# Placing a group's output stage inside the second batch's attention, and transposing the late batches' rows on TensorE

## The chip, the cores and the metric

The kernel runs on one core of one Trainium2 chip. The metric is device microseconds of that core; three runs of the kernel before gave 349.78, 351.61 and 352.11 us, with the median at 351.61.

## The reference

For each of 8 batches and 8 heads (576 tokens, head dimension 64) the reference computes causal attention with a window of 128 tokens and a linear position bias, then feeds the rows to a two-layer block with a gated activation:

```python
scores = scale * (q @ k.T) + slope[h] * -(i - j)      # only 0 <= i - j < 128
attn   = softmax(scores);  x = attn @ v               # heads side by side: 4608 x 512
h      = x @ w_in                                     # 512 x 2048
out    = (h / (1 + exp(-beta * h))) @ w_out           # 2048 x 512
```

## The kernel before, in words

**Tiling.** The 4608 token rows form 9 groups of 512 (`TOKG`). A group needs 16 H items (`HS(g, j)`: four matmuls of 128x512 through `W1`, L507, then a tanh on ScalarE, L514, and a gate on VectorE, L515, into `gts[g]`) and 16 O items (`OS(g, i, n)`: four matmuls through `W2`, L530, for row block i; the fourth item of a block also scales it into `osb` on ScalarE, L536). A finished block is stored by `store()`, L543, nearly always from GpSimd's queue. The H items read the transposed attention output `XT`, a ring of three groups.

**Attention.** Batches 0 and 1 work on head pairs: `TP` transposes q and k on TensorE (L288), `SP_` forms scores in the PSUM tile `SS` and takes the exponential (L341), `PVP` multiplies with v (L364) and normalizes, `XP` puts the pair into `XT` (L375). The visit "A" of a pair covers the first two query blocks, and "B" query blocks 2 and 3, which read key and v blocks 1, 2 and 3. The last 64 rows of a batch have steps of their own, `tail(b)`: `TT`, `SCT`, two `PV` and `X`. Batches 2 to 7 have q and k transposed by DMA (`DT`, L403), scores by `SC` (L424, exponentials L434, mask L438), `PV` (L459, L463, L348, L349), and `X`, which carries a block of rows into `XT`. For batches below `XDMA` = 4, X is four TensorE transposes into PSUM (L482) and a copy on VectorE (L488); from batch 4 on it is one DMA transpose, issued by SyncE (L477).

**Loads.** `get` and `get_pair` issue q, k and v from SyncE's queue into the `fst` buffers (13 of them). GpSimd casts them to bf16: `cast_pair`, `cast_qk` (L252, L253) and `cast_v` (L265). GpSimd's queue also loads the weights with a cast on the way (`load_w1`, L272; `load_w2`, L276: four pieces of four O steps each), makes the masks (`constants_masks`, L195) and issues the stores.

**What sets the order.** TensorE, SyncE and GpSimd execute in exactly the order in which the program emits their instructions; ScalarE's and VectorE's order is written out only for the opening, and is planned by the framework after that. After the opening, batch 1's attention and batch 0's last rows (the list `second`, 23 steps) are spread over the H items 3 to 15 of group 0. Then comes group 1: its H items with all O items of group 0 and the first half of its own, `tail(1)` and batch 2's loads (`jobs(2)`) in between. From there on each group g has its 16 H items, half of the O items of group g-1 and half of its own; `spread` sets the steps of the batches 2 to 7 (`att`) between them by weight, from item `first` to item `last`, so that the rows of the next group are complete in time (`need`).

Of the kernel before, what the change touches and what calls it, by code (L numbers as in the profile page):

```python
# [15 lines left out]
P = 128  # L16
# [3 lines left out]
def kernel(  # L20
# [10 lines left out]
    nc = tc.nc  # L31
# [7 lines left out]
    NQB = 5  # L39
# [8 lines left out]
    qscale = 1.0 / sqrt(D)  # L48
    REF = 63.5
    FAR = 1.0e5  # L50
    XDMA = 4

    const = ctx.enter_context(tc.tile_pool(name="const", bufs=1))
    ident = const.tile([P, P], BF16, name="ident")
# [26 lines left out]
    fst_pool = ctx.enter_context(tc.tile_pool(name="fst", bufs=13))  # L81
    bst_pool = ctx.enter_context(tc.tile_pool(name="bst", bufs=4))
    pt_pool = ctx.enter_context(tc.tile_pool(name="ptp", bufs=10))
    xn_pool = ctx.enter_context(tc.tile_pool(name="xn", bufs=4))
    gt_pool = ctx.enter_context(tc.tile_pool(name="gt", bufs=2))
    sig_pool = ctx.enter_context(tc.tile_pool(name="sig", bufs=3))
    osb_pool = ctx.enter_context(tc.tile_pool(name="osb", bufs=4))
# [187 lines left out]
    def load_w2(n):  # L275
        return nc.gpsimd.dma_start(  # L276
            out=W2[:, bass.ts(n, 4), :], in_=W2v[:, bass.ts(n, 4), :])
# [191 lines left out]
    def X(b, qb):  # L469
        nq = ROWS[qb]  # L470
        xnv = xns.pop((b, qb))[:].rearrange("p h d -> p (h d)")
        if b >= XDMA:
            tok0 = (b * S + P * qb) % XTR
            n1 = min(nq, XTR - tok0)
            for r0, r1, at in ((0, n1, tok0), (n1, nq, 0)):
                if r0 < r1:
                    nc.sync.dma_start(  # L477
                        out=XT[:, :, at : at + r1 - r0], in_=xnv[r0:r1], transpose=True)
            return
        xt = psum_t.tile([P, NDM, P], BF16, name="xt", tag="t")  # L480
        for c in range(NDM):
            nc.tensor.transpose(  # L482
                out=xt[:, c, 0:nq], in_=xnv[0:nq, c * P : (c + 1) * P],
                identity=ident[0:nq, 0:nq]
            )
# [33 lines left out]
    def HS(g, j):  # L519
        Hm(g, j, range(NDM))  # L520
# [37 lines left out]
    def pvx(b, qbs):  # L558
        r = []
        for qb in qbs:  # L560
            r += [(None, lambda g=g, qb=qb: PV(b, qb, g), 2) for g in range(2)]
            if b >= XDMA:
                r.append(((b, qb), lambda qb=qb: X(b, qb), 0))
            elif qb != qbs[0]:
                r.append(((b, qb - 1), lambda qb=qb: X(b, qb - 1), 2))
        if b < XDMA:
            r.append(((b, qbs[-1]), lambda: X(b, qbs[-1]), 2))
        return r

    def merged(a, c):  # L570
# [35 lines left out]
    with tc.manual_schedule(engines={ENG.PE, ENG.SP, ENG.Pool}):  # L606
# [66 lines left out]
        for n in range(1, NP):  # L673
            get_pair(1, n)
            if n == 1:
                get("v", 1, 0)
                get("v", 1, 1)
        get("v", 1, 2)
        get("v", 1, 3)
        for b in range(2):  # L680
            for w in "qkv":
                get(w, b, 4)
        cast_pair(1, 0)
        cast_pair(1, 1)
        cast_v(1, 0)
# [2 lines left out]
        w2 = [load_w2(0), load_w2(1)]  # L688
        cast_pair(1, 3)
        w2 += [load_w2(2), load_w2(3)]  # L690
        cast_v(1, 2)
        cast_v(1, 3)
        for b in range(2):
            cast_qk(b, 4)
            cast_v(b, 4)
        constants_masks()
        second = [
            lambda: TP(1, 0), lambda: SP_(1, "A", 0), lambda: (TP(1, 1), SP_(1, "B", 0)),
            lambda: SP_(1, "A", 1), lambda: PVP(1, "A", 0), lambda: (TP(1, 2), SP_(1, "B", 1)),
# [3 lines left out]
            lambda: (XP(1, 1), PVP(1, "B", 2)), lambda: PVP(1, "A", 3), lambda: XP(1, 2),  # L703
            lambda: PVP(1, "B", 3), lambda: XP(1, 3),
        ] + tail(0)
        done = 0
        for j in range(3, NFF):
            HS(0, j)
            to = len(second) * max(0, j + 1 - 5) // (NFF - 5)
            while done < to:  # L710
                second[done]()
                done += 1


        work = tail(1)
        b2 = jobs(2)
        after_w2 = [True]
        for n in range(5):
            s, j = b2.pop(0)
            r = j()  # L720
            if after_w2[0]:
                after_w2[0] = False
                after(r[0], w2[1])
        OG = lambda g, i: [lambda n=n: OS(g, i, n) for n in range(4)]
        HG = lambda g: [lambda j=j: HS(g, j) for j in range(NFF)]
        h = HG(1)
        items = h[:4]
        o = OG(0, 0) + OG(0, 1) + OG(0, 2) + OG(0, 3) + OG(1, 0) + OG(1, 1)
        for n in range(12):
            items += [h[4 + n]] + o[n : n + 1]  # L730
        items += o[12:]
        done, dw, dj = 0, 0, 0

        def spread(items, first, last, target):
# [13 lines left out]
        def wrap(it, n):  # L748
            def f():
                nonlocal dw, dj  # L750
                it()
                while dw < min(len(work), len(work) * (n + 1) // 10):
                    work[dw]()
                    dw += 1
                while dj < min(len(b2), len(b2) * (n + 1) // 24):
                    b2[dj][1]()
                    dj += 1
            return f

        spread([wrap(it, n) for n, it in enumerate(items)], 17, len(items) - 2, need[2])  # L760
        for g in range(2, NTG):
            h = HG(g)
            o = OG(g - 1, 2) + OG(g - 1, 3)
# [41 lines left out]
```

The softmax here doesn't subtract the row's maximum and nothing guards it: scores larger than these inputs give would overflow.

## Time and profile before

| | |
|---|---|
| median of three runs | 351.61 us (349.78 to 352.11) |
| profiled execution | 352.11 us, span of the instructions 350.1 us |
| PE busy | 324.5 us, 93% of the span |
| DVE / ACT / POOL busy | 192.3 / 206.9 / 111.5 us |
| H matmuls, L507, on `hps` | 560 recorded, 382 ns each |
| O matmuls, L530 | 576, 379 ns each |
| X on TensorE, L482 | 48 matmuls, from 60.5 to 154.8 us |
| X by DMA, L477 | 21 DMA transposes, from 163.4 to 305.7 us |
| stores from GpSimd's queue | 34 of 256 KB |

In the profile PE is TensorE's matmuls, PEld its weight loads, DVE VectorE, ACT ScalarE, POOL GpSimd, SP SyncE; a name such as L507 is a line of the kernel. A busy time counts the modelled lengths of matmuls, which overlap in a stream: in the chain of waits, four matmuls of 512 columns in a row follow each other within 0.86 us. A row of a timeline gives the start and the length in us, engine, line, operation, output and inputs with their shapes, and in brackets the idle time ahead of it with what ended it. The slices of the page divide the span into 40 equal parts, one digit (tenths) each.

### The profile page before, as it was taken

The numbers are of one execution on the slowest core, as the hardware profiler recorded it, in microseconds if no ns is written. First come the engines' busy times: TensorE is split into PE (matmuls) and PEld (weight loads), VectorE is DVE, ScalarE is ACT, GpSimd is POOL, SyncE is SP. The second block draws the span as 40 slices with busy tenths as digits, with TensorE's granted clock in tenths as the row PEclk, the third lists the DMA queues.
The fourth block names the chain that finished last, engine by engine and source line by source line (L and its number), as shares of the span: only waits on it lengthen the run. The fifth ranks groups of instructions, "written<-read, shape, count | busy, mean of one in ns | idle before, by whom it ended". The sixth has DMA issues, their size and how long they took to land.

```text
span 350.1 us, 6218 instructions
## 1 busy us (share of the span) xinstructions
PE 324.5 (93%) x2289; PEld 151.4 (43%) x2289; DVE 192.3 (55%) x422; ACT 206.9 (59%) x396; POOL 111.5 (32%) x208
## 2 busy tenths in 40 slices
PE   6886886998999999998999999999999999999995
PEld 2442443443444444443444444444444444544442
DVE  7445576454754776476627763674477455614500
ACT  2545663548856776566657775675687566426511
POOL 4793624633735333503131324242200100010010
PEclk9899999899999999999999999999999999999999
DMA  7998999999999999991286989799311201120012
GB/s 176 228 195 204 194 186 202 177 201 220 217 230 237 239 211 226 212 198 48 57 182 133 182 175 227 129 222 166 93 32 53 77 30 47 30 99 0 30 62 90
DMA packets 152285, 51.79 MB, mean 148 GB/s; under 512 B 143664, under 2 KB 149824, under 8 KB 152256
## 3 DMA queue, kind: packets, MB, share of 16 engines
q1 hardware_dynamic: 145312, 38.30, 57.5%
q0 software_dynamic: 6944, 13.11, 14.9%
q8 instruction: 18, 0.29, 0.4%
q14 instruction: 11, 0.09, 0.1%
HBM read 36.71 MB, written 9.44 MB: 132 GB/s over the span
## 4 chain that ended last, share of the span: by engine, by line
PE 67%; ACT 11%; DVE 10%; DMA 6%; issue 3%; SPq 3%; POOL 0%; POOLq 0%; ACTq 0%
PE ops L530 31%; PE hps L507 26%; ACT pt L434 8%; DVE gT L515 4%; DVE pt L438 4%; PE SS L424 3%; DMA W<-in_moe_w_in_dram 3%; ACT sig L514 2%; SPq L234 2%; DMA fst<-in_k_dram 2%; PE pv L463 2%; PE pv L459 1%; DMA fst<-in_q_dram 1%; DVE xn L349 1%; PE SS L324 1%
## 5 line engine op out<-in xcount | busy, mean ns | idle before, releaser
L507 PE MATMUL hps<-XT,W 128*128 128x512 bf16 x560 | 141.5, 382 | 5.6 <-DVE gT L515 4.0
L530 PE MATMUL ops<-W,gT 128*128 128x512 bf16 x576 | 139.0, 379 | 0.0
L515 DVE SCALAR_TENSOR_TENSOR gT<-sig,hps 128x512 bf16<-128x512 bf16 x140 | 94.7, 683 | 76.4 <-ACT sig L514 75.7
L514 ACT ACTIVATE sig<-hps,beta_h 128x512 bf16<-128x512 f32 x140 | 95.8, 694 | 61.4 <-PE hps L507 56.1
L434 ACT ACTIVATE pt<-SS,bias 128x256 bf16<-128x256 f32 (+1 forms) x192 | 75.0, 478 | 11.4 <-PE SS L424 11.3
L507 PEld LDWEIGHTS <-W 128*128 128x128 bf16 x576 | 51.5, 98 | 62.6 <-issue 11.8
L530 PEld LDWEIGHTS <-gT 128*128 128x128 bf16 x576 | 52.4, 98 | 58.1 <-issue 2.1
L543 POOL DMA_DIRECT2D out_dram<-osb x34 | 18.4, 542 | 136.2 <-ACT osb L536 134.4
L438 DVE TENSOR_TENSOR pt<-pt,mask 128x1024 bf16<-128x1024 bf16 x48 | 38.0, 792 | 26.7 <-ACT pt L434 26.7
L536 ACT ACTIVATE osb<-ops 128x512 f32<-128x512 f32 x36 | 21.6, 600 | 44.6 <-PE ops L530 44.6
L265 POOL CAST vs<-fst 128x512 bf16<-128x512 f32 (+1 forms) x40 | 25.0, 636 | 37.4 <-DMA fst<-in_v_dram 32.5
L252 POOL CAST bst<-fst 128x512 bf16<-128x512 f32 (+1 forms) x32 | 20.7, 647 | 32.5 <-DMA fst<-in_q_dram 22.9
L349 DVE TENSOR_TENSOR xn<-pv,zs 128x256 bf16<-128x256 f32 (+1 forms) x64 | 26.9, 421 | 1.7
L348 DVE RECIPROCAL zs<-pv 128x4 f32<-128x4 f32 (+1 forms) x80 | 14.0, 176 | 22.3 <-PE pv L463 13.3
L253 POOL CAST bst<-fst 128x512 bf16<-128x512 f32 (+1 forms) x32 | 21.0, 656 | 10.2 <-DMA fst<-in_k_dram 10.0
L463 PE MATMUL pv<-vs,pt 128*128 128x65 bf16 x240 | 21.4, 193 | 0.0
L424 PE MATMUL SS<-qkT 64*128 64x256 bf16 (+2 forms) x240 | 18.9, 252 | 2.6 <-ACT pt L434 2.4
L463 PEld LDWEIGHTS <-pt 128*128 128x128 bf16 x240 | 16.5, 97 | 8.4
L341 ACT ACTIVATE pt<-SS 128x768 bf16<-128x768 f32 (+1 forms) x12 | 10.6, 881 | 15.5 <-PE SS L335 15.4
L424 PEld LDWEIGHTS <-qkT 64*128 64x128 bf16 x240 | 8.4, 94 | 23.1 <-issue 22.7
L459 PE MATMUL pv<-vs,pt 128*128 128x65 bf16 x192 | 17.9, 193 | 0.0
L459 PEld LDWEIGHTS <-pt 128*128 128x128 bf16 x192 | 15.2, 98 | 5.6
(78 smaller groups left out, 148.5 us busy)
## 6 DMA issues: line engine op xcount, KB each, us to landing
out_dram<-osb POOLq DMA_DIRECT2D x34, 256.0 KB, 3.3
fst<-in_q_dram SPq DMA_DIRECT2D x32, 256.0 KB, 4.8
fst<-in_v_dram SPq DMA_DIRECT2D x32, 256.0 KB, 4.0
fst<-in_k_dram SPq DMA_DIRECT2D x24, 256.0 KB, 5.2
fst<-in_k_dram SPq DMA_DIRECT2D x24, 128.0 KB, 4.0
W<-in_moe_w_in_dram POOLq DMA_DIRECT2D x4, 512.0 KB, 9.5
W<-in_moe_w_out_dram POOLq DMA_DIRECT2D x4, 512.0 KB, 11.1
fst<-in_q_dram SPq DMA_DIRECT2D x8, 128.0 KB, 3.3
```

What stands on the lines that cost most here:

```text
L265: return nc.gpsimd.tensor_copy(out=VS[b % 2][0:rows, sb, :, 0:D], in_=fs.pop(("v", b, sb))[0:rows])
L349: nc.vector.tensor_tensor(out=xn, in0=pv[0:nq, :, 0:D], in1=zs[0:nq].broadcast_to([nq, 4, D]), op=ALU.mult)
L424: nc.tensor.matmul(o, lhsT=qk[64 * e : 64 * e + 64, 1, p, P * kb : P * kb + P], rhs=qk[64 * e : 64 * e + 64, 0, p, P * kb : P * kb + nq], ...
L434: nc.scalar.activation(out=pt[:, e, cols], in_=sps[:, e, cols], func=ACTF.Exp, scale=qscale, bias=bias[:, half, h : h + 1],)
L438: nc.vector.tensor_tensor(out=pt[:], in0=pt[:], in1=masks[m][:], op=ALU.mult)
L459: nc.tensor.matmul(pv[:, hl, 0 : D + 1], lhsT=weights(b, qb - 1, h, 1), rhs=vs[:, qb - 1, h, 0 : D + 1], start=True, stop=False,)
L463: nc.tensor.matmul(pv[:, hl, 0 : D + 1], lhsT=weights(b, qb, h, 0), rhs=vs[:, qb, h, 0 : D + 1], start=qb == 0, stop=True,)
L507: nc.tensor.matmul(hps[:], lhsT=W1[:, c, bass.ts(j, P)], rhs=XT[:, c, c0 : c0 + TOKG], start=(c == 0), stop=(c == NDM - 1),)
L514: nc.scalar.activation(out=sig[:], in_=hps[:], func=ACTF.Tanh, scale=beta_h[:, j : j + 1])
L515: nc.vector.scalar_tensor_tensor(out=gts[g][:, j, :], in0=sig[:], scalar=1.0, in1=hps[:], op0=ALU.add, op1=ALU.mult)
L530: nc.tensor.matmul(ops_, lhsT=gT[:, j, i * P : i * P + P], rhs=W2[:, j, :], start=(j == 0), stop=(j == NFF - 1),)
L536: nc.scalar.mul(osb[:], ops_, 0.5)
```

## The change

- `second` is spread over 21 items in place of 13: H items 3 to 15 of group 0, and then the eight O items of its row blocks 0 and 1, alternating. Finished blocks are stored there.
- Group 1 has its 16 H items with the eight O items of group 0's row blocks 2 and 3 between them, and then the first half of its own O items. `att` starts after item 10 in place of 17.
- SyncE issues q, k, v of batch 0's last rows ahead of the last two v blocks of batch 1, and GpSimd casts in the same order; the masks are made ahead of batch 1's first cast.
- Batch 2's ten q and k loads are issued in one go; its casts, DMA transposes and v loads follow in a list of their own, spread over group 1.
- X is done on TensorE and VectorE for all batches; `XDMA` and the DMA transposes of `X` are gone. `att` now ends three items before a group's end in every group, where it was seven in the groups with X by DMA.
- `xn` has 3 buffers in place of 4.

```diff
-    XDMA = 4
...
-    xn_pool = ctx.enter_context(tc.tile_pool(name="xn", bufs=4))
+    xn_pool = ctx.enter_context(tc.tile_pool(name="xn", bufs=3))
...
     def X(b, qb):
         nq = ROWS[qb]
         xnv = xns.pop((b, qb))[:].rearrange("p h d -> p (h d)")
-        if b >= XDMA:
-            tok0 = (b * S + P * qb) % XTR
-            n1 = min(nq, XTR - tok0)
-            for r0, r1, at in ((0, n1, tok0), (n1, nq, 0)):
-                if r0 < r1:
-                    nc.sync.dma_start(
-                        out=XT[:, :, at : at + r1 - r0], in_=xnv[r0:r1], transpose=True)
-            return
...
             r += [(None, lambda g=g, qb=qb: PV(b, qb, g), 2) for g in range(2)]
-            if b >= XDMA:
-                r.append(((b, qb), lambda qb=qb: X(b, qb), 0))
-            elif qb != qbs[0]:
+            if qb != qbs[0]:
                 r.append(((b, qb - 1), lambda qb=qb: X(b, qb - 1), 2))
-        if b < XDMA:
-            r.append(((b, qbs[-1]), lambda: X(b, qbs[-1]), 2))
+        r.append(((b, qbs[-1]), lambda: X(b, qbs[-1]), 2))
...
+        for w in "qkv":
+            get(w, 0, 4)
         get("v", 1, 2)
         get("v", 1, 3)
-        for b in range(2):
-            for w in "qkv":
-                get(w, b, 4)
+        for w in "qkv":
+            get(w, 1, 4)
+        constants_masks()
         cast_pair(1, 0)
...
         w2 += [load_w2(2), load_w2(3)]
+        cast_qk(0, 4)
+        cast_v(0, 4)
         cast_v(1, 2)
         cast_v(1, 3)
-        for b in range(2):
-            cast_qk(b, 4)
-            cast_v(b, 4)
-        constants_masks()
+        cast_qk(1, 4)
+        cast_v(1, 4)
+        for sb in range(NQB):
+            r = get("q", 2, sb)
+            if sb == 0:
+                after(r, w2[1])
+            get("k", 2, sb)
...
+        fills = HG(0)[3:]
+        for n in range(4):
+            fills += [OG(0, 0)[n], OG(0, 1)[n]]
         done = 0
-        for j in range(3, NFF):
-            HS(0, j)
-            to = len(second) * max(0, j + 1 - 5) // (NFF - 5)
+        for n, f in enumerate(fills):
+            f()
+            to = len(second) * max(0, n - 2) // (len(fills) - 3)
             while done < to:
                 second[done]()
                 done += 1
+            if waiting:
+                store()
...
-        items = h[:4]
-        o = OG(0, 0) + OG(0, 1) + OG(0, 2) + OG(0, 3) + OG(1, 0) + OG(1, 1)
-        for n in range(12):
-            items += [h[4 + n]] + o[n : n + 1]
-        items += o[12:]
+        o = OG(0, 2) + OG(0, 3)
+        items = []
+        for n in range(8):
+            items += h[2 * n : 2 * n + 2] + o[n : n + 1]
+        items += OG(1, 0) + OG(1, 1)
...
-                while dj < min(len(b2), len(b2) * (n + 1) // 24):
-                    b2[dj][1]()
+                while dj < min(len(b2), len(b2) * (n + 2) // 20):
+                    b2[dj]()
                     dj += 1
...
-        spread([wrap(it, n) for n, it in enumerate(items)], 17, len(items) - 2, need[2])
+        spread([wrap(it, n) for n, it in enumerate(items)], 10, len(items) - 2, need[2])
...
-            late_x = TOKG * (g + 2) > XDMA * S
-            spread(items, 0, len(items) - (7 if late_x else 3), target)
+            spread(items, 0, len(items) - 3, target)
```

More of the change, by code (lines that the diff above doesn't have):

```diff
@@ L705 @@
         ] + tail(0)
+        OG = lambda g, i: [lambda n=n: OS(g, i, n) for n in range(4)]
+        HG = lambda g: [lambda j=j: HS(g, j) for j in range(NFF)]
+        fills = HG(0)[3:]
+        for n in range(4):
+            fills += [OG(0, 0)[n], OG(0, 1)[n]]
         done = 0
-        for j in range(3, NFF):
-            HS(0, j)
-            to = len(second) * max(0, j + 1 - 5) // (NFF - 5)
+        for n, f in enumerate(fills):
+            f()
+            to = len(second) * max(0, n - 2) // (len(fills) - 3)
             while done < to:
@@ L712 @@
                 done += 1
+            if waiting:
+                store()
         work = tail(1)
[L716 to L725, printed above, removed]
-        h = HG(1)
-        items = h[:4]
-        o = OG(0, 0) + OG(0, 1) + OG(0, 2) + OG(0, 3) + OG(1, 0) + OG(1, 1)
-        for n in range(12):
-            items += [h[4 + n]] + o[n : n + 1]
-        items += o[12:]
+        b2 = []
+        for sb in range(NQB):
+            b2 += [lambda sb=sb: cast_qk(2, sb), lambda sb=sb: DT(2, sb)]
+            if sb:
+                b2.append(lambda sb=sb: get("v", 2, sb - 1))
+            if sb > 1:
+                b2.append(lambda sb=sb: cast_v(2, sb - 2))
+        b2 += [lambda: get("v", 2, 4), lambda: cast_v(2, 3), lambda: cast_v(2, 4)]
+        h = HG(1)
+        o = OG(0, 2) + OG(0, 3)
[3 more added lines that the diff above has]
+        items += OG(1, 0) + OG(1, 1)
         done, dw, dj = 0, 0, 0
```

## The prediction

> **What bounds the kernel now.** I read the page's slices first, then the busy times by stage, then the waits and the timelines of the stage that the change rewrites. Columns of the second block: stretch, length, busy time (instructions) of PE, PEld, DVE, ACT, POOL, then the clock, DMA share, GB/s.
>
> ```profile
> PE   6886886998999999998999999999999999999995
> PEclk9899999899999999999999999999999999999999
> ...
> 29.40:61.70 32.30, 23.72 (x248) 12.09 (x247) 19.25 (x47) 16.05 (x21) 15.40 (x27) 1.00 1.07 193
> 61.70:66.30 4.60, 4.60 (x20) 1.77 (x20) 1.71 (x3) 1.37 (x2) 4.32 (x14) 0.63 0.85 151
> 81.00:90.00 9.00, 6.57 (x43) 2.58 (x42) 4.80 (x7) 8.04 (x20) 4.74 (x8) 1.00 1.09 233
> 90.00:144.00 54.00, 53.72 (x425) 25.77 (x421) 35.00 (x78) 36.47 (x82) 24.08 (x39) 1.00 1.17 222
> 144.00:304.00 160.00, 155.73 (x1066) 72.15 (x1065) 96.17 (x193) 106.38 (x218) 34.97 (x59) 1.00 0.58 120
> ```
>
> From 90 us on PE is the bound: 0.3 us idle in 54, then 4.3 in 160. The loose stage is 29.4 to 61.7, batch 1's attention between the H items of group 0: 8.6 us of plain idle, and 11.2 us if every matmul is priced at its spacing in a full stream (0.216 us for 512 columns) instead of its recorded length. At its end the clock falls to 0.63.
>
> **What the Trainium skill says.** (1) "DMA: Bandwidth & Descriptors", section "Queues, rings and completion order": each DMA engine goes round robin between the rings that have work, a packet at a time. The trace agrees, and this decides my forecast. W2 is issued from POOL at 39.63 to 43.8. Between 42.5 and 56.5 us its queue (q0) and SP's (q1) moved nearly equally many packets, of 1024 and of 256 bytes, so that SP's loads got a quarter of the bytes:
>
> ```profile
> q0 software_dynamic: 2032, 2.02, 87.4%
> q1 hardware_dynamic: 2404, 0.60, 30.6%
> ```
>
> SP's queue carried 1.11 MB in the 5 us from 36 to 41, and 0.60 MB in these 14 us. (2) "TensorE: Matmul & The Clock Gate", section "Part 1: The HAM clock gate": after an idle window of some 3.4 us the clock halves, and about as long a busy window brings it back. The trace: eight matmuls in 2.95 us at 61.70, against 1.73 for eight in a full stream. (3) The same page, "Part 4: PE-mode transpose": the transposed block lands in PSUM and needs a copy. Here that copy is L488, 0.42 us on DVE.
>
> **The fill stage.** New order: the steps of `second` are spread over 13 H items and 8 O items; SP loads q, k, v of (0,4) ahead of v(1,2) and v(1,3), and POOL casts in that order. Before, v(1,2) and v(1,3) were issued at 36.31 and 37.89 and landed at 41.48 and 42.24, just as W2 began. What came after them shows in POOL's casts, which wait for landings:
>
> ```profile
> 39.63 1.57 POOL L276 DMA_DIRECT2D W<-in_moe_w_out_dram  x2
> ...
> 43.77 1.18 POOL L265 CAST vs<-fst 128x512 bf16<-128x512 f32 x2
> 47.35 0.61 POOL L252 CAST bst<-fst 64x512 bf16<-64x512 f32 x1 [2.40 <-PE xtp L375]
> 50.77 0.61 POOL L253 CAST bst<-fst 64x512 bf16<-64x512 f32 x1 [2.80 <-DMA fst<-in_k_dram]
> 54.65 0.61 POOL L265 CAST vs<-fst 64x512 bf16<-64x512 f32 x1 [3.28 <-DMA fst<-in_v_dram]
> 57.97 0.61 POOL L252 CAST bst<-fst 64x512 bf16<-64x512 f32 x1 [2.71 <-DMA fst<-in_q_dram]
> ```
>
> These are q, k, v of (0,4) and q of (1,4): 128 KB each, one per 3.1 to 3.9 us while W2 runs. Now count bytes behind the last q of pair 3. Before: 512 KB (the two v) by 42.24, 640 by 47.2, 768 by 50.7, 896 by 54.6. After: 384 KB (the three of (0,4)) and half of v(1,2) by 42.2, v(1,2) whole at 640 KB, so 47.2, v(1,3) at 896 KB, so **54.6**. With its cast (0.6) and the wake-up, PE can run the step PVP(1,B,0), which reads key blocks 1 to 3, at 55.3.
>
> When does PE get there? Before, at 44.88:
>
> ```profile
> 31.61 0.40 PE L288 MATMUL tps<-ident,bst 128*128 128x128 bf16 x4 [1.79 <-POOL bst L258]
> ...
> 44.88 0.42 PE L364 MATMUL pv<-vs,pt 128*128 128x65 bf16 x8
> 45.13 1.02 PE L507 MATMUL hps<-XT,W 128*128 128x512 bf16 x4
> ```
>
> After, four more H items stand ahead of it (through H(0,13) instead of H(0,9)): 4 x 0.86 = 3.5 us, of which the waits that they cover (about 3.1 of the 4.9 lost from 29.4 to 44.9) come back: 45.3. So PE waits **10.0 us**, with everything behind it in its order, O items included. The rest after it: six PVP 1.4, H(0,14) and (0,15) 1.7, two score steps 1.55, four XP 0.9, eight O items 8 x 0.86 = 6.9, TT and SCT 1.2, two PV 0.5, and the last transpose with its DVE chain as before (59.34 to 61.70) 2.4: 16.6. Small waits 0.3. The idle 10 us halves the clock; at one window of 3.4 us that costs 1.7. H(1,0) then starts at 55.3 + 16.6 + 0.3 + 1.7 = 73.9. Before it started at 61.70, with 6.9 of these O items and 1.8 of half clock and waits (61.7 to 66.3) to come: 70.4. **Fill stage: +3.5 us.** Bounds: v(1,3) 2 us earlier or later, +1.5 to +5.5.
>
> **Smaller edits.** `constants_masks` goes ahead of cast_pair(1,0) on POOL: 14 selects, 3.76 us in one row, into a gap of 3.95 us (26.9 to 30.95) that waits for k: nothing, at worst 0.4 us if it overruns. Batch 2's ten q, k loads in one go (six before) queue behind v(1,4): W2 is over, so they land at about 1.2 us each, 60 to 70, and nothing behind them is due before H(1). Their casts stand on POOL behind the two new stores of O(0,0) and O(0,1), so wait for ACT's osb at about 72, yet the first scores of batch 2 come ten items on, at about 84: covered. With the stretch 81 to 90 (three waits for ACT's exponentials on the single SS, 2.4 us idle) unchanged in kind, but two H items in three instead of one in two, ACT has a little more: +0.3 (0 to +1.5). Three `xn` buffers instead of four: a row block's X follows the next block's PV, so two live at a time: nothing.
>
> **X of batches 4 to 7.** Off SP: 21 DMA transposes. Onto PE: 16 blocks of four 128-column transposes and 4 blocks of 64. PE's price is start to start:
>
> ```profile
> 100.09 0.39 PE L482 MATMUL xt<-ident,xn 128*128 128x128 bf16 x4
> 100.31 1.03 PE L530 MATMUL ops<-W,gT 128*128 128x512 bf16 x4
> ```
>
> 0.22 us a block; 16 x 0.224 + 4 x 0.14 = **4.1 us** on the bound engine. DVE gets 21 copies, some 8.5 us in 160, and was busy 96: beside PE's work. Against it: these stages lose 6.3 us by full-stream prices (3.6 of it waits of hps for DVE's gT), while group 2 (109.3 to 144.5), which already transposes on PE, lost 0.8. With X on DMA the attention is pressed into 25 of a group's 32 items; now it gets 29, as group 2 has. Five groups at 0.8 would be 4; I count on 4.3, so -2.0 (0 to -4): **+2.1** net, bounds 0 to +4.5.
>
> **Sum.** 3.5 + 0.3 + 2.1 = +5.9 on the span of 350.1, 356.0; with the 2.0 us around it (352.11 less 350.1) 358.0. The profiled execution was 0.5 above the median of the three shown, so **357.5**.
>
> **Rivals.** (a) On the other side: **v(1,3) lands before PE wants it.** For it: SP issues these loads before W2's, and the smaller three take 128 KB fewer than the two v. Against: the byte count above. Without the wait H(1,0) starts at 45.3 + 16.6 + 0.3 = 62.2, 8.2 us ahead of 70.4; with +2.4 for the rest, 345.8. It decides once v(1,3) lands before about 50. (b) Half way: v(1,3) gets through one W2 chunk earlier, at 51: wait 6, clock 1.7, fill -0.5, total +1.9, 353.5. (c) Slower still: X's copies queue ahead of gT on DVE and the late stages keep all their 6.3 us, or batch 2's casts hold its scores: +3 to +5 more, 362.
>
> **Chances.** Forecast 0.62, (a) 0.12, (b) 0.17, (c) 0.09. Within 1% (3.5 us, about what a measurement of this kernel tells from no change) lie most of (b) and the low edge of the forecast: 0.21. Faster 0.11, slower 0.68. The range, 349.5 to 362.5, leaves out (a) and the upper half of (c).
>
> **What would show it.** Right: PE waits for POOL's vs at L364 for about 10 us near 45 to 55, POOL's L265 before it ends a wait for in_v at about 54.6, the clock drops after, H(1,0) starts near 74, and L482 has 128 matmuls. Wrong: v(1,3) cast by 46 and O rows at about 52 to 58, or late stages longer than before by more than 4 us.

## The result, and the profile after

The changed kernel takes 368.16 us at the median of four runs (364.46 to 368.61), the kernel before 350.69 us beside it: a ratio of 1.047, with a 95% interval of 1.039 to 1.055. It is slower, as forecast, but by 17.5 us where 5.9 were predicted, and lies outside the range given. The profiled execution took 368.41 us with a span of 366.4 us, 16.3 more than the span before. The changed file is shorter, so a line has a number that is smaller by 1 in its first part and by 9 further on: the matmul of PVP is L363, POOL's cast of v L264, the H and O matmuls L498 and L521, the scores of SC L423, the gate L506, X on PE L473. One of the experiments (e4) had TensorE's clock at 0.75 from 67 us on in its profiled execution and was made again as e4b, and the profiled executions of e2, e4b and e8 were 4.2, 3.5 and 4.4 us slower than the medians of their runs, so that their lengths of stages are those of a slow run.

The slices of the page (40 of 9.16 us each) show where PE has now become idle, in the sixth slice, and where its clock falls:

```profile
PE   7789807988879999998998999999999999999994
PEclk9999965999998999999999999999999999999999
```

Before, the sixth slice stood at 8, and the clock was nearly full there. The busy times by stage, in the columns that the prediction uses (stretch, length, busy time and instructions of PE, PEld, DVE, ACT, POOL, clock, DMA share, GB/s), for the fill up to the wait, the wait, the rest of the fill, the end of group 1 and the late groups 3 to 7:

```profile
30.70:44.70 14.00, 13.35 (x115) 6.56 (x116) 8.99 (x20) 9.68 (x13) 9.55 (x16) 1.00 0.97 193
44.70:57.75 13.05, 0.67 (x10) 0.46 (x9) 0.65 (x2) 1.02 (x1) 1.91 (x4) 0.67 1.14 193
57.75:75.96 18.21, 17.12 (x155) 8.52 (x154) 9.32 (x24) 5.37 (x7) 2.95 (x6) 0.86 0.65 138
107.00:115.00 8.00, 5.47 (x41) 2.70 (x40) 2.63 (x8) 2.02 (x5) 4.00 (x7) 0.79 1.18 222
155.60:327.80 172.20, 167.24 (x1186) 79.04 (x1184) 105.72 (x217) 108.54 (x220) 34.98 (x61) 1.00 0.44 100
```

The same stretch of the late groups in the kernel before:

```profile
145.50:312.60 167.10, 162.83 (x1105) 75.52 (x1104) 97.47 (x196) 108.01 (x220) 36.05 (x61) 1.00 0.56 117
```

Up to 44.7 us the denser order does what it promises: PE is idle for 0.65 us in 14. Then it does next to nothing for 13 us. The late groups are 5.1 us longer, with 4.4 more of PE's busy time and 0.7 more idle; in these stretches the H matmuls wait 4.6 us for the gate, and 3.6 before. PE's waits of the kernel after (what waited, for what; us in total, times, longest):

```profile
PE pv L363 <- POOL vs L264: 12.4, 2, 8.9
PE hps L498 <- DVE gT L506: 5.5, 7, 1.7
PE SS L423 <- DMA qkT<-bst: 2.5, 1, 2.5
```

Neither the first nor the third was among the six largest before; the second was 4.0 us. The rows of the timeline around the long wait, and those around the third wait:

```profile
37.48 1.57 POOL L275 DMA_DIRECT2D W<-in_moe_w_out_dram  x2
...
53.10 0.61 POOL L264 CAST vs<-fst 128x512 bf16<-128x512 f32 x1 [6.11 <-DMA fst<-in_v_dram]
53.76 0.38 PE L363 MATMUL pv<-vs,pt 128*128 128x65 bf16 x4 [8.90 <-POOL vs L264]
56.95 0.62 POOL L264 CAST vs<-fst 128x512 bf16<-128x512 f32 x1 [3.24 <-DMA fst<-in_v_dram]
57.62 0.32 PE L363 MATMUL pv<-vs,pt 128*128 128x65 bf16 x3 [3.48 <-POOL vs L264]
57.75 1.90 PE L498 MATMUL hps<-XT,W 128*128 128x512 bf16 x4
...
75.96 1.89 PE L498 MATMUL hps<-XT,W 128*128 128x512 bf16 x8 [0.38 <-DVE XT L479]
...
109.91 0.28 PE L423 MATMUL SS<-qkT 64*128 64x256 bf16 x2 [2.53 <-DMA qkT<-bst]
```

v(1,2) lands at 53.05 and v(1,3) at 56.90; each is cast as soon as it lands, and PE's next two matmul groups follow within 0.1 us of the cast's end. Four H matmuls at 57.75 then take 1.90 us instead of 1.03: half clock. H(1,0) starts at 75.96. The queues' traffic from 42 to 56 us, after:

```profile
q0 software_dynamic: 1854, 1.83, 78.3%
q1 hardware_dynamic: 3668, 0.92, 42.1%
```

W2 (q0) moves twice the bytes of SP's loads (q1) while SP's loads are what PE waits for. As long as both have work, the packets go one to one: 624 and 625 from 46 to 50 us. W2's last packets leave at about 54 us, and SP's queue then moves 0.42 MB from 54 to 56. A second stretch shows the opposite, DMA engines with nothing to do, at the end of the fill:

```profile
66.50:78.50 12.00, 10.91 (x109) 5.63 (x106) 5.28 (x15) 3.46 (x5) 3.75 (x7) 1.00 0.26 74
```

Their share is 0.26, where the kernel before has 1.06 from 66.3 to 109.3. The waits of SP's queue from 60 to 110 us say why:

```profile
SPq L402 <- POOL bst L252: 17.2, 3, 11.1
```

The rows of POOL and SP at the end of this wait:

```profile
73.89 0.56 POOL L534 DMA_DIRECT2D out_dram<-osb  x1 [14.27 <-ACT osb L527]
75.31 0.56 POOL L534 DMA_DIRECT2D out_dram<-osb  x1 [0.86 <-ACT osb L527]
...
76.42 0.62 POOL L252 CAST bst<-fst 128x512 bf16<-128x512 f32 x1
...
77.07 1.33 SPq L402 DMA_TRANSPOSE qkT<-bst  x1
```

SP's last issue ahead of this ends at 66.5. Then SP stands at the first DMA transpose of batch 2, which needs POOL's cast of k, until 77.1 (the view counts 11.1 us). POOL made that cast at 76.42, since two stores stood ahead of it in its order; the first waited 14.3 us for ACT's osb, until 73.89.

To place the loss I cut both traces at the first tanh of each group. Lengths in us; "end" is from the start of group 8 to the end of the span. The two O row blocks that moved from group 1 to group 0 are 6.9 us of full-stream work, so the second row shows the kernel before as if they had been moved.

| | start | group 0 | group 1 | group 2 | groups 3 to 7 | end | span |
|---|---|---|---|---|---|---|---|
| before | 26.5 | 36.5 | 47.4 | 35.2 | 167.1 | 37.5 | 350.1 |
| before, O items moved | 26.5 | 43.4 | 40.5 | 35.2 | 167.1 | 37.5 | 350.1 |
| after | 26.4 | 50.7 | 43.5 | 35.1 | 172.2 | 38.6 | 366.4 |

The 16.3 us are 10.2 up to the end of group 1, 5.1 in groups 3 to 7, and 1.1 at the end, less 0.1 in group 2. The 1.1 us at the end are not PE's: counted from the cut, its last matmul ends at 33.63 and the last store is issued at 34.34 in both kernels, and the difference comes after that. The kernels with the stores at the places of the kernel before, those with the stores on ACT's queue, and e15 end at 37.3 to 37.8, all others but e4 at 38.0 to 38.7; what makes the difference isn't shown.

### The profile page after: what moved, and what is told of

Same layout as the page of the kernel before. It is cut to its first block, busy times and chain, and to the rows that moved or that the text cites. A ratio compares the mean times of both kernels' runs of the same rounds, so it can differ in the third digit from the quotient of the medians.

```text
span 366.4 us, 6341 instructions
## 1 busy us (share of the span) xinstructions
PE 330.1 (90%) x2369; PEld 155.5 (42%) x2369; DVE 201.7 (55%) x443; ACT 207.3 (57%) x396; POOL 109.8 (30%) x208
## 3 DMA queue, kind: packets, MB, share of 16 engines
q1 hardware_dynamic: 135424, 35.93, 49.8%
## 4 chain that ended last, share of the span: by engine, by line
PE 62%; DMA 12%; DVE 6%; POOL 6%; ACT 4%; SPq 4%; issue 4%; POOLq 0%; ACTq 0%
PE ops L521 30%; PE hps L498 24%; DMA fst<-in_q_dram 5%; DMA fst<-in_v_dram 5%; DVE pt L437 3%; ACT pt L433 3%; PE SS L423 3%; DVE gT L506 2%; PE pv L462 2%; SPq L233 1%; PE pv L458 1%; SPq L223 1%; PE xt L473 1%; DMA qkT<-bst 1%; POOL tablet L179 1%
## 5 line engine op out<-in xcount | busy, mean ns | idle before, releaser
L498 PE MATMUL hps<-XT,W 128*128 128x512 bf16 x560 | 142.0, 383 | 7.2 <-DVE gT L506 5.5
L521 PE MATMUL ops<-W,gT 128*128 128x512 bf16 x576 | 142.6, 382 | 0.0
L506 DVE SCALAR_TENSOR_TENSOR gT<-sig,hps 128x512 bf16<-128x512 bf16 x140 | 94.8, 683 | 64.3 <-ACT sig L505 63.5
L498 PEld LDWEIGHTS <-W 128*128 128x128 bf16 x576 | 51.4, 98 | 63.0 <-issue 14.1
L521 PEld LDWEIGHTS <-gT 128*128 128x128 bf16 x576 | 51.3, 98 | 53.5 <-issue 2.0
L437 DVE TENSOR_TENSOR pt<-pt,mask 128x1024 bf16<-128x1024 bf16 x48 | 40.6, 845 | 22.7 <-ACT pt L433 22.4
L527 ACT ACTIVATE osb<-ops 128x512 f32<-128x512 f32 x36 | 21.7, 603 | 43.2 <-PE ops L521 43.2
L264 POOL CAST vs<-fst 128x512 bf16<-128x512 f32 (+1 forms) x40 | 25.4, 642 | 40.9 <-DMA fst<-in_v_dram 39.7
L251 POOL CAST bst<-fst 128x512 bf16<-128x512 f32 (+1 forms) x32 | 19.9, 621 | 11.0 <-DMA fst<-in_q_dram 6.3
L423 PE MATMUL SS<-qkT 64*128 64x256 bf16 (+2 forms) x240 | 19.1, 252 | 4.2 <-DMA qkT<-bst 2.5
L462 PE MATMUL pv<-vs,pt 128*128 128x65 bf16 x240 | 21.6, 195 | 0.0
L252 POOL CAST bst<-fst 128x512 bf16<-128x512 f32 (+1 forms) x32 | 20.0, 625 | 4.2 <-DMA fst<-in_k_dram 4.2
L423 PEld LDWEIGHTS <-qkT 64*128 64x128 bf16 x240 | 8.1, 94 | 24.9 <-issue 24.6
L363 PE MATMUL pv<-vs,pt 128*128 128x65 bf16 x112 | 6.6, 199 | 13.1 <-POOL vs L264 12.4
L458 PE MATMUL pv<-vs,pt 128*128 128x65 bf16 x192 | 18.3, 195 | 0.0
```

The source lines that it names most:

```text
L264: return nc.gpsimd.tensor_copy(out=VS[b % 2][0:rows, sb, :, 0:D], in_=fs.pop(("v", b, sb))[0:rows])
L423: nc.tensor.matmul(o, lhsT=qk[64 * e : 64 * e + 64, 1, p, P * kb : P * kb + P], rhs=qk[64 * e : 64 * e + 64, 0, p, P * kb : P * kb + nq], ...
L437: nc.vector.tensor_tensor(out=pt[:], in0=pt[:], in1=masks[m][:], op=ALU.mult)
L458: nc.tensor.matmul(pv[:, hl, 0 : D + 1], lhsT=weights(b, qb - 1, h, 1), rhs=vs[:, qb - 1, h, 0 : D + 1], start=True, stop=False,)
L462: nc.tensor.matmul(pv[:, hl, 0 : D + 1], lhsT=weights(b, qb, h, 0), rhs=vs[:, qb, h, 0 : D + 1], start=qb == 0, stop=True,)
L498: nc.tensor.matmul(hps[:], lhsT=W1[:, c, bass.ts(j, P)], rhs=XT[:, c, c0 : c0 + TOKG], start=(c == 0), stop=(c == NDM - 1),)
```

## The experiments

Two questions were put to the chip. First: is the loss in the fill the order of the loads, and is it W2's packets that hold v back? The rival was that the denser order itself costs time there. Second, when the late v was cured and most of the gain still failed to appear: is group 1 held by the order of the steps on the queues, or by the rate at which the DMA engines move the bytes? The letters in the expectations stand for the theories of that run, and each says what it means by them. "Before" in brackets is the kernel before on the same chip.

| | edit | median, us (before) | ratio, 95% interval | group 0 | group 1 | groups 3 to 7 |
|---|---|---|---|---|---|---|
| e7 | after, again | 364.12 (351.41) | 1.034 (1.024 to 1.044) | 48.1 | 43.2 | 172.2 |
| e1 | after, v(1,2) and v(1,3) first | 355.32 (350.31) | 1.017 (1.012 to 1.021) | 36.0 | 45.7 | 172.1 |
| e2 | after, X of batches 4 to 7 by DMA | 356.92 (350.31) | 1.018 (1.014 to 1.022) | 48.8 | 43.3 | 166.9 |
| e3 | before, loads' order of after | 365.17 (350.31) | 1.040 (1.032 to 1.048) | 50.5 | 46.4 | 167.3 |
| e4b | before, all X on PE | 357.75 (351.41) | 1.012 (1.006 to 1.019) | 40.4 | 46.4 | 172.2 |
| e5 | e1 and e2 together | 353.27 (351.41) | 1.004 (1.001 to 1.007) | 35.4 | 50.4 | 167.2 |
| e6 | after, W2 behind v(1,3) | 357.52 (351.41) | 1.013 (1.008 to 1.018) | 38.3 | 44.6 | 172.2 |
| e8 | e5, batch 2's steps as before | 350.18 (351.47) | 0.997 (0.995 to 1.000) | 41.9 | 44.1 | 167.0 |
| e12 | e5, batch 2's casts ahead of its v | 351.32 (351.47) | 1.002 (0.999 to 1.004) | 39.7 | 43.3 | 167.1 |
| e9 | before, stores from ACT's queue | 354.68 (351.47) | 1.012 (1.007 to 1.017) | 36.8 | 49.9 | 166.6 |
| e10 | e8, stores from ACT's queue | 350.74 (351.47) | 0.999 (0.996 to 1.001) | 41.7 | 41.5 | 166.6 |
| e13 | e8, v(1,2), v(1,3) ahead of pair 3 | 350.59 (351.29) | 0.999 (0.997 to 1.001) | 35.9 | 44.9 | 167.3 |
| e14 | e12, the same | 351.18 (351.29) | 0.999 (0.997 to 1.002) | 35.5 | 47.6 | 167.3 |
| e15 | e13, no stores of rows 0 to 767 | 347.04 (351.29) | 0.987 (0.982 to 0.992) | 38.8 | 39.1 | 167.2 |

Lengths of groups are those of each kernel's one profiled execution, cut at ACT's tanh; in e10 ACT stood at a store ahead of the first tanh of group 1, so that some 6 us of its group 0 belong to group 1 by PE's order. In e3, e4b and e9, which are the kernel before with one edit, the two moved O row blocks still lie in group 1; in all others they lie in group 0.

### e1: the two v blocks first

```diff
-        for w in "qkv":
-            get(w, 0, 4)
         get("v", 1, 2)
         get("v", 1, 3)
+        for w in "qkv":
+            get(w, 0, 4)
...
-        cast_qk(0, 4)
-        cast_v(0, 4)
         cast_v(1, 2)
         cast_v(1, 3)
+        cast_qk(0, 4)
+        cast_v(0, 4)
```

> The changed kernel with one edit: v(1,2) and v(1,3) are loaded and cast ahead of q, k, v of (0,4) again, as before the change. Theory A (the late v costs the fill stage): PE's wait of 12.4 us for POOL's casts of v goes, and most of the half clock from 49 to 63 us with it; the first sig of group 1 comes near 64 to 66 us in place of 77.0, and the time falls by 10 to 13 us, to 355 to 358. Rival B (the wait only moves: then q, k, v of (0,4) land behind W2, at about 55, and TT and PV of (0,4) wait for them): less than 5 us are won, 363 or more.

The wait for v is gone, and H(1,0) starts at 60.83 instead of 75.96. The time falls by 12.8 us against the first runs of the changed kernel, 8.8 against e7's. So the denser order costs nothing in the fill; the loads' order does, and q, k and v of (0,4), which now come behind, hold PE nowhere (rival B). But a wait that stood at 2.5 us in the kernel after has grown:

```profile
PE SS L423 <- DMA qkT<-bst: 4.4, 4, 1.8
```

These are scores that wait for a DMA transpose of q and k, in group 1.

### e2: X of the late batches by DMA again

```diff
+    XDMA = 4
...
+        if b >= XDMA:
+            ... (the DMA transposes of the kernel before)
+            return
...
-            spread(items, 0, len(items) - 3, target)
+            late_x = TOKG * (g + 2) > XDMA * S
+            spread(items, 0, len(items) - (7 if late_x else 3), target)
```

(`xn` has 4 buffers again.)

> The changed kernel with one edit: X of the batches 4 to 7 is a DMA transpose again, with attention ending seven items ahead in those groups and four xn buffers. Theory A (each X costs PE its 0.22 us and nothing is won back): 4 to 5.5 us less than the changed kernel, 363 to 364, the gain all in groups 4 to 6. Rival B (as I predicted: the longer stretch for the attention wins back half of it): 1 to 3 us less, 365 to 367.

Groups 3 to 7 return to 166.9 us, 5.3 less than in the kernel after. That is the part which the edit explains. The median fell by 11.2 against the first runs of the kernel after and 7.2 against e7's; the 2 us or more that are left over aren't placed. The profiled execution, 361.12, has a fill as long as e7's; of the three faster runs (355.20 to 357.17), whose fill may have been shorter, there is no trace.

### e3: the loads' order alone

```diff
+        for w in "qkv":
+            get(w, 0, 4)
         get("v", 1, 2)
         get("v", 1, 3)
-        for b in range(2):
-            for w in "qkv":
-                get(w, b, 4)
+        for w in "qkv":
+            get(w, 1, 4)
...
+        cast_qk(0, 4)
+        cast_v(0, 4)
         cast_v(1, 2)
         cast_v(1, 3)
-        for b in range(2):
-            cast_qk(b, 4)
-            cast_v(b, 4)
+        cast_qk(1, 4)
+        cast_v(1, 4)
```

> The kernel before with one edit: q, k, v of (0,4) loaded and cast ahead of v(1,2) and v(1,3). Theory A (the order alone brings the wait; O items have no part in it): PE waits some 9 to 12 us at L364 for POOL's vs from about 45 us; since TT and PV of (0,4) no longer have to wait and other waits of this stage are swallowed, the time grows by 5 to 9 us, to 356 to 360. Rival B (it takes the O items and the tighter sequence of the changed kernel for the order to hurt): within 2 us of the kernel before.

14.9 us slower, where theory A gave 5 to 9: this one edit is enough for the long wait, without the O items. It isn't a share of the change's 17.5 us, in which the moved O items win back some 8 us of the fill (group 0 takes 35.4 us in e5, and 43.4 in the kernel before with its O items moved). Its largest wait on PE:

```profile
PE pv L364 <- POOL vs L265: 12.2, 2, 7.1
```

Of the cost, 12.2 are that wait; the clock was at half for 17.1 us, from 47.2 to 64.3.

### e4 and e4b: X on PE alone

```diff
-    XDMA = 4
+    XDMA = 8
```

> The kernel before with one edit: XDMA = 8, so that X of all batches is on PE and DVE, and the attention ends three items before each group's end. Theory A: 20 blocks cost 4.1 us of PE and the late stages lose as much to waits as before: 354.5 to 356. Rival B (a calmer sequence wins back two thirds, as group 2 suggested): 351.5 to 353.

364.07 us at the median, with 358 to 365 in its three other runs: not read, as said above. Again:

> The kernel before with XDMA = 8 once more, since the profiled execution of the first try ran at a clock of 0.75 throughout and its times spread over 5 us. Theory A: the groups 3 to 7 take 4.5 to 5.5 us more together than in the kernel before, nothing else changes: 354.5 to 356. Rival B (X on PE costs beyond its matmuls, by half-clock windows in the later stages): 358 or more.

357.75. Groups 3 to 7 take 172.2 us, 5.1 more than before, exactly as in the kernel after. The profiled execution had a 3.5 us wait for v in its fill, whose program is that of the kernel before: W2 was issued at 36.15, right behind the last v at 36.09, where the kernel before had 39.63 and 37.89. That is scatter of the fill and not X. The median lies above theory A's 356; the 1 us or so beyond the 5.1 isn't placed.

### e7: the kernel after once more

> The changed kernel itself, next to the other three on one chip, so that e2 and e4 can be set against it. Theory A (the profiled e2 tells the truth: X by DMA takes 5.3 us from groups 4 to 8, the rest of e2's 11 us is the fill stage's scatter from run to run): about 362 to 368 with a scatter of some 4 us. Rival B (X on PE costs 10 us or more in all): 366 to 369 with little scatter.

364.12 us, with a wait for v of 9.7 us (v(1,3) landed at 54.49), and H(1,0) at 73.17. W2 was issued at 35.93, 1.6 us sooner than in the first profiled execution, and v(1,3) 1.3 us sooner; W2's last packets left at about 52 in place of 54. So one program gives some 3 us more or less in this stage; what decides it isn't shown.

### e5: v first and X by DMA

The edits of e1 and e2 together.

> The changed kernel with both taken back: v(1,2), v(1,3) first (e1), and X of the batches 4 to 7 by DMA (e2). What is left of the change: the O items in the fill stage, batch 2's loads at once, the masks earlier. Theory A (costs add as the traces of e1 and e2 show): e1's 355.3 less 5.3, 350, with its waits of PE for qkT (4.4 us) still there. Rival B (e2's median counts in full): 344 to 346.

Still not faster than before. Group 0 took 35.4 us, where the kernel before takes 43.4 with its O items moved, so 8.0 us were won there; group 1 then took 50.4 us, ten more than the 40.5 of the kernel before with its O items moved:

```profile
PE SS L424 <- DMA qkT<-bst: 8.2, 3, 4.1
```

with the clock at half from 75.2 to 82.0 and from 99.1 to 105.9. POOL stands for 8.87 us at a cast of v:

```profile
75.95 0.61 POOL L265 CAST vs<-fst 128x512 bf16<-128x512 f32 x1 [8.87 <-DMA fst<-in_v_dram]
```

POOL's next two casts, at 76.51 and 77.07, are of q and k. What is won in the fill comes back as waits of PE for q and k, in part through this order on POOL (e12, below, changes it).

### e6: W2 behind the last v

```diff
-        w2 = [load_w2(0), load_w2(1)]
         cast_pair(1, 3)
-        w2 += [load_w2(2), load_w2(3)]
         cast_qk(0, 4)
         cast_v(0, 4)
         cast_v(1, 2)
         cast_v(1, 3)
+        w2 = [load_w2(n) for n in range(4)]
```

> The changed kernel, its order of loads kept (q, k, v of (0,4) ahead of v(1,2), v(1,3)), but all four pieces of W2 are issued by POOL after the cast of v(1,3). Theory A (W2's packets take the turns of SP's loads): v(1,3) lands at about 42 to 43 in place of 56.9, PE's wait at L363 falls from 12.4 us to under 1; W2 lands at about 48 to 60 and O items wait for it for 2 to 5 us; the time falls by 8 to 12 us. Rival B (v(1,3) is late because of its place behind three more loads): it lands after 50 as before, and the time grows, as W2 comes later still.

With the loads in the order of the change, but W2 issued when v(1,3) has been cast:

```profile
43.71 0.61 POOL L264 CAST vs<-fst 128x512 bf16<-128x512 f32 x1 [0.23 <-DMA fst<-in_v_dram]
44.27 3.05 POOL L275 DMA_DIRECT2D W<-in_moe_w_out_dram  x4
```

v(1,3) lands at 43.66, 13.2 us earlier than in the kernel after, with as many bytes ahead of it on its own queue. So the 384 KB ahead don't make v late by themselves, and W2 by itself makes no wait in e1 and one of 3.5 us at most in the other runs with v first (e4b): the long wait takes both, the place behind these loads and W2's packets in the way. PE then waits 1.5 us for W2 at the first O items. 6.6 us less than e7, 10.6 less than the first runs; theory A gave 8 to 12.

### e8 and e12: batch 2's casts sooner

e8 takes batch 2's steps from `jobs(2)` as before, at a quicker pace; e12 leaves the list and puts its casts of q and k ahead of v's loads.

```diff
-        b2 = []
-        ...
+        b2 = jobs(2)
...
-                while dj < min(len(b2), len(b2) * (n + 2) // 20):
-                    b2[dj]()
+                while dj < min(len(b2), len(b2) * (n + 2) // 16):
+                    b2[dj][1]()
```

> e5 (v first, X by DMA) with batch 2's loads, casts, DMA transposes in the order of the list jobs(2) as before the change, at a pace of 16 items. Theory A (the order of SP's and POOL's queues in the new list makes PE wait for qkT in group 1: ten loads ahead of the first DMA transpose, casts of v ahead of casts of q, k): the 8.2 us that PE waits for qkT fall under 3, the group's half-clock windows go, and the time is 344 to 348. Rival B (the loads of the batches 2 and 3 come at the rate of the DMA engines, so that the 8 us won in the fill stage must be given back): the waits stay above 5 us, 350 to 354.

```diff
-            if sb:
-                b2.append(lambda sb=sb: get("v", 2, sb - 1))
-            if sb > 1:
-                b2.append(lambda sb=sb: cast_v(2, sb - 2))
-        b2 += [lambda: get("v", 2, 4), lambda: cast_v(2, 3), lambda: cast_v(2, 4)]
+        for sb in range(NQB):
+            b2.append(lambda sb=sb: get("v", 2, sb))
+            if sb:
+                b2.append(lambda sb=sb: cast_v(2, sb - 1))
+        b2.append(lambda: cast_v(2, 4))
```

> e5 with one edit: in batch 2's list all five casts of q, k with their DMA transposes stand ahead of the loads and casts of v; the ten loads stay at once. Theory A: POOL's wait for v(2,0) no longer holds the casts of q, k of (2,3) and (2,4), nor those of batch 3; PE's waits for qkT fall from 8.2 to about 4, since the first two, behind the ten loads, stay; 348 to 351. Rival B (rate of the DMA engines): no change, 352 to 354.

350.18 and 351.32 us, some 3 and 2 us better than e5, each against the kernel before beside it. e8's interval is clear of e5's, so the order on the queues was worth something; e12's overlaps it. Both kernels now stand level with the kernel before. Waits remain in both (qkT 3.7 and v 2.9 in e8; 2.7 and 2.4 in e12): theory A of e8 was right that the waits would shrink, and wrong that the time would fall to 348 or less.

### e9 and e10: stores from ACT's queue

```diff
-        eng = nc.sync if row0 >= B * S - 2 * P else nc.gpsimd
+        eng = nc.sync if row0 >= B * S - 2 * P else nc.scalar
```

> The kernel before with one edit: all stores but the last two are issued from ACT's queue in place of POOL's. Theory A (POOL, held at each store until ACT has made osb, catches up with runs of casts back to back, and VectorE's bf16 multiply L438 stands still as long as such a run lasts, PE then waits for gT): L438 above 1 us becomes rare (7 of 48 in the kernel before), PE's waits for gT in groups 3 to 7 fall from 3.6 to under 2 us, and the time falls by 1 to 3 us. Rival B (runs of casts come from loads that land together, or ACT loses more by issuing): no change or slower by up to 3 us.

> e8 with the stores from ACT's queue as in e9. Theory A (POOL's waits at the stores also hold the casts of batch 3 in group 1): 1 to 3 us less than e8 and PE's waits for qkT near 0. Rival B: as e8.

The stores, which hold POOL's casts while they wait for ACT's osb, are off POOL. In the kernel before this costs 1.2%: PE's waits for gT grow from 4.0 to 6.2 us, because ACT now stands at the stores. In e8's order, the waits for qkT are gone, and SP's longest stand at a DMA transpose falls from 8.5 to 2.1 us, so the stores on POOL had held the loads there. But the waits for gT grow from 4.2 to 8.9: ACT stands at the first two stores (issued at 64.51 and 67.18), the next tanh comes at 67.92, and PE waits 5.0 us. The sum is 350.74, no change.

### e13, e14 and e15: v ahead of pair 3, and without the early stores

```diff
         for n in range(1, NP):
+            if n == 3:
+                get("v", 1, 2)
+                get("v", 1, 3)
             get_pair(1, n)
...
-        get("v", 1, 2)
-        get("v", 1, 3)
```

> e8 (v ahead of (0,4), X by DMA, batch 2's steps from jobs(2)) with v(1,2), v(1,3) loaded even ahead of pair 3 of batch 1, so that they land before W2 starts. Theory A (order): PE's wait for v (2.9 us in e8) and the half-clock window of 6.8 us after it go, the fill stage shrinks from 41.9 to 36 us as in e5, group 1 stays at 44: 344 to 347, faster than the kernel before. Rival B (rate of the DMA engines): the fill stage shrinks just so, but group 1 grows by as much, by waits for qkT: 349 to 352.

> e12 (ten loads at once, casts of q, k ahead of those of v) with v(1,2), v(1,3) ahead of pair 3. Theory A: the wait for v goes, fill 36, and the waits for qkT grow a little, from 2.7 to about 5: 346 to 349. Rival B: 350 to 352.

PE no longer waits for v in either, the fill is 35.9 and 35.5 us, and the total still doesn't move: 350.59 and 351.18. The waits for qkT are 4.5 and 4.8 us. e15 is e13 without the stores of output rows 0 to 767 (1.5 MB), which therefore stay unwritten:

```diff
         row0, osb = waiting.pop(0)
+        if row0 < 2 * TOKG - 2 * P:
+            return
```

> e13 without the stores of the first 768 rows (group 0 and the first half of group 1, 1.5 MB of writes; those rows of the output stay unwritten). At 200 GB/s that is 7 us of the DMA engines' time in group 1, and POOL never waits for osb there. Theory A (order alone): within 1.5 us of e13. Rival B (rate of the DMA engines): PE's waits for qkT shrink by several us and the time is 3 to 6 us below e13.

347.04, 3.5 us less than e13, and no wait for qkT at all. The stretch from 70 to 80 us, in e13:

```profile
70.00:80.00 10.00, 6.34 (x32) 2.13 (x29) 3.59 (x8) 5.22 (x12) 3.14 (x6) 0.87 1.07 203
```

and in e15:

```profile
70.00:80.00 10.00, 8.49 (x60) 3.65 (x58) 5.75 (x11) 6.77 (x15) 4.91 (x8) 1.00 1.10 219
```

The DMA engines' share is about the same in both (1.07 and 1.10); PE is busy for 2.2 us more of the ten. Group 1 falls from 44.9 to 39.1 us. This fits the rate of the DMA engines, but doesn't prove it. The fill of that one execution is 2.9 us longer, mostly in waits for loads ahead of 50 us, before any store is due, so the loads had 2.9 us more to run ahead of PE, about the length of e13's first wait (3.0 us, ending at 75.90). Only two of the six stores, 0.5 MB, had been issued in e13 by then. The end of the kernel, behind all of PE's work, is 1.0 us shorter too. And POOL's casts no longer stand behind these stores. Between the bytes and POOL's waits e10 doesn't decide, since there PE stood for ACT instead. What is shown is that these stores cost some 3.5 us in all.

## Why the prediction was wrong

**The late v: right in kind and near in size, in part by luck.** The prediction had PE at PVP(1,B,0) at 45.3 and v(1,3) at 54.6, a wait of 10.0. Measured: PE stood still from 44.9; v(1,3) landed at 56.90 in the kernel after and at 54.49 in e7; the waits were 12.4 and 9.7. The Trainium skill's page "DMA: Bandwidth & Descriptors", section "Queues, rings and completion order", has engines take a packet from each ring in turn; the one to one count of packets above agrees, and so does e6: with W2 out of the way v(1,3) landed at 43.66. e3 confirms that the loads' order brings the wait by itself. But the count of bytes was off on the way: it had all of (0,4) and half of v(1,2) in by 42.2 and v(1,2) at 47.2, and v(0,4) came at 46.3 and v(1,2) at 53.05. W2 was issued at 37.48, 2.1 us sooner than in the trace that the count was made on, since the last q ahead of it landed sooner, and so caught v(0,4) as well. It was also through sooner, at about 54 in place of 56, and v(1,3) followed within 3 us, in e7 as here. The two errors nearly cancel in v(1,3). H(1,0), predicted at 73.9, started at 75.96 and at 73.17 (e7): the fill's +3.5 measured +5.6 and +2.8, inside its bounds but for 0.1 us.

**"At one window of 3.4 us that costs 1.7": too small.** The clock's record stands at half for 13.7 us, from 49.2 to 62.8. PE was busy for 5.6 of these, which costs about 2.8 us.

**"The first scores of batch 2 come ten items on, at about 84: covered", and so group 1 at +0.3: the step that failed most.** The prediction saw the casts of batch 2 stand on POOL behind the two new stores until about 72 (measured: the first store went at 73.89), and asked only when batch 2's own scores are due. Those were indeed in time. But the DMA transpose that follows each cast is issued by SP, and SP's order holds batch 2's v and the loads of batch 3 behind it: no load was issued for 10.5 us, and what was late was the batch after. The score step at 107.1 to 109.9 waits 2.5 us for the third DMA transpose of batch 3, which SP issued at 105.6, having issued one DMA after the other without a gap since 92.5. This chain is read from the trace; no run took the two stores alone out of it (e10, with all stores but the last two off POOL in another order of steps, lost both SP's long stand and this wait). The idle time starts a window of half clock (110.6 to 114.0) that costs about 1.7 more. From H(1,0) to the end of group 1 the kernel after needs 4.6 us more than the kernel before with the same items (10.2 later at its end, less the fill's 5.6; the prediction's 70.4 counts the half clock at 62 us to the fill); e7 needs 4.3 more. The other waits of this stretch come to about as much as before, so some 0.4 us isn't placed.

Why a wait for qkT stays when v is early (e1, e5, e13) is open in part. The order of steps on the queues has a share, some 3 us of e5 by e8. The rest may be the rate of the DMA engines, whose share is 0.94 to 1.25 in every stretch of 8 or 10 us from 62 to 110 us in these three; e15 fits that, and can't tell it from POOL's waits and from its own longer fill.

**"So -2.0" for fewer waits in the late groups: wrong in sign.** X cost its 4.1 us of full-stream time, as the sum has it (128 X matmuls on PE, as expected). The waits, by full-stream prices, didn't fall by 2.0 but rose by 1.0: +5.1 in groups 3 to 7, in the kernel after, in e1, e4b, e6 and e7 alike, and -5.3 when X went back (e2). So the step that failed is the credit for a looser spread of the attention, 29 items in place of 25. What PE waits for in these groups is the gate: 3.6 us before and 4.6 after, with the looser spread. Four of the five waits after, 4.3 us, come behind a mask multiply of VectorE that took 1.2 to 2.3 us in place of 0.69 (last section). In one of the four a copy of X stands ahead of the multiply on VectorE. The looser spread, the matmuls of X and its copies changed together in every run, so that their shares in the waits aren't told apart. Late stages longer by more than 4 us were among the prediction's own signs of being wrong.

**The masks and the `xn` buffers: right, at nothing.** The masks are made from 26.4 to 30.2, and the cast behind them starts at once; no wait for a free `xn` is among PE's or VectorE's.

**The rivals.** (a), 345.8 if v were early, was built as e1. Its step about the fill was right: H(1,0) at 60.8 against the 62.2 given. Its total was not: 355.3, and still 353.3 and 350.6 in e5 and e13, which take X's loss out as well. It counted the gain in the fill as a gain in time, and group 1 then grew, from 40.5 to 45.7 us in e1, by waits for qkT and the clock after them. (b), half way, is disproved by the landing times. (c), 362, named the late stages keeping their waits, or batch 2's casts holding its scores, +3 to +5 *more*; the first of these happened in full, though not shown to be for its reason, and the second one batch further on. No rival reached the measured time. The measured terms are the fill +5.6, group 1 +4.6, the late groups +5.1 and the end +1.1, for which the prediction had no term, less 0.1 in group 2: 16.3.

## What to carry over

When a load is put behind others, look for a second queue that is about to start: the packets that take turns with it set the price, and a place 384 KB further back cost a wait of 12 us here, but none with W2 held back. When a step is held on one queue, follow it through every queue that has a step waiting for it, to the loads behind that step; the damage shows a batch later than the step's own use. And before a wait is said to go because work is spread more thinly, read what that wait is made of.

## What the runs showed that was not expected

**A mask multiply can stand still behind a run of casts.** VectorE's mask multiply (L438 before, L437 after, 128x1024 bf16) takes 0.69 us when no cast of POOL overlaps it (28 of 48 before, 33 of 48 after), and up to 2.6 us when some do: 0.94 us on average over the other 20 before, 1.19 over the other 15 after. A long one, in the timeline of the kernel after:

```profile
191.82 2.33 DVE L437 TENSOR_TENSOR pt<-pt,mask 128x1024 bf16<-128x1024 bf16 x1 [0.77 <-ACT pt L433]
191.88 0.61 POOL L252 CAST bst<-fst 128x512 bf16<-128x512 f32 x1
192.44 0.61 POOL L251 CAST bst<-fst 128x512 bf16<-128x512 f32 x1
193.00 0.61 POOL L252 CAST bst<-fst 128x512 bf16<-128x512 f32 x1
194.80 1.02 PE L498 MATMUL hps<-XT,W 128*128 128x512 bf16 x4 [1.69 <-DVE gT L506]
```

It ends 0.54 us after the last cast of the run (193.61), and the other seven over 1 us in this kernel end 0.54 to 0.55 us after theirs; the gate behind it is late, and PE waits 1.69 us. The Trainium skill, "SBUF — State Buffer", section "SBUF: two separate sides", says that a VectorE operation with two SBUF inputs and a GpSimd operation exclude each other for an instruction's whole length. The trace agrees with the exclusion, but here VectorE lost its turn to several casts in a row, not to one. That is read from the traces; no kernel without these casts was run. e9 was to thin out the runs of casts by taking the stores off POOL. The multiplies over 1 us fell from 7 to 3 of 48 and PE's longest wait for the gate in groups 3 to 7 from 1.7 to 0.9 us, but these waits came to 3.5 us together, against 3.6 before, so theory A of e9 (under 2) was wrong; ACT stood at the stores in this kernel, and its share isn't told apart.

**Short idle times of PE can cost clock as well.** The 2.5 us wait at 107 us was followed by 3.4 us at half clock, all of it over work. Single waits of 2.6 us in e8, 2.7 in e12 and 3.0 in e13 brought such a window as well; one of 1.5 us in e13, at 96 us, didn't. Waits of 8.2 us in e5 brought two windows of 6.8 us with 10.0 us of work in them. Four H matmuls at half clock took 1.90 us and 1.03 at full clock, so about half of the work's time in such a window is lost. With this loss the wait of the kernel after cost 1.7 times its own length, and those of e5 1.6 times.
